# Two packed matmul blocks moved next to each other at the end of four L2 phases

## The chip, the cores and the metric

The kernel runs on one core of one Trainium2 chip. The metric is the device time of one execution in microseconds (us). A run counts as slow when it took over 1.5% longer than the fastest of its kernel, and as fast otherwise. The sets of experiments ran on different chips, so totals are compared only with runs of before in the same rounds.

## The reference

Linear attention with the feature map elu + 1 on 8 batches of 8 heads (576 positions, 64 values per head), then a gated feed-forward block.

```python
q_p, k_p = phi(q), phi(k)                       # phi = elu + 1
kv  = np.einsum('bhsd,bhse->bhde', k_p, v)      # "k.v" below
z   = np.sum(k_p, axis=2)
num = np.einsum('bhsd,bhde->bhse', q_p, kv)     # "q.kv" below
den = np.einsum('bhsd,bhd->bhs', q_p, z)[..., None] + 1e-06
x   = (num / den), heads side by side           # 4608 tokens x 512
out = (silu(x @ w_gate) * (x @ w_val)) @ w_out  # "L1" is the first two products, "L2" the last
```

## The kernel before

The 4608 tokens are handled in 9 groups of 512. For group g, L1 makes 12 blocks of hidden units and L2 multiplies them with w_out. L2 uses the seven-product scheme of fast matrix multiplication. Each product exists twice (`tt` = 0 and 1, two token halves), so L2 is 14 steps of six 128x256 matmuls. Results gather in four half-used PSUM banks. The two "x banks" are `pX[0]`, `pX[1]` and the two "z banks" are `pX[2]`, `pV[2]`. Between the products, VectorE and ScalarE read partial sums out: `k1`, `k2`, `k5` are copies by ScalarE, `c11`, `c22`, `c12` drains by VectorE.

While L2 of group g runs, TensorE also does two small jobs for later groups, as packed 64x64 matmuls (four tiles of the array at once):

- **q.kv** of the next group (`mm2`, 16 matmuls for two batches) fills the four banks `pV[1]`, `pG[1]`, `pV[0]`, `pG[0]`. These are copied to `xT`, which L1 of the next group reads. ScalarE copies two of them and VectorE two.
- **k.v** of the batch after that (`joint`, 72 matmuls) fills parts of two banks, `kvb[b]`. VectorE makes `zd` from them and ScalarE `R`.

```python
    def mm1(b, lp):
        if lp == 0:
            kvb[b] = ((pV[2], pX[0]), (pX[2], pV[2]), (pX[0], pX[1]), (pV[0], pG[0]), (pV[1], pG[1]))[min(b, 4)]
        for j in range(J):
            ...                                   # (cut) for hh in 0, 1
                    for e in range(2):
                        nc.tensor.matmul(
                            out=kvb[b][hh][D * e:D * e + D, 256 * lp:256 * lp + D + 1],
                            lhsT=term_[rows, j, P * lp + D * e:P * lp + D * e + D],
                            rhs=vm[b % 2][rows, j, 2 * lp + e, :], start=(j == 0), stop=(j == J - 1))

    def mm2(g, ps, engs):                         # (cut)
        for b in sorted(set(u[0] for u in us)):
            ...
                corners([x[:, c0:c0 + C * len(js)] for x in ps], kv(b), b, js[0], js[-1] + 1)
        for i in range(4):                        # the xT copies
            ...

    # l2_steps(g), the list of steps for groups 2 to 6: p[n][tt] is product n of half tt
            return [(p[1][0],), (p[1][1], k1[0]), (p[2][0], k1[1]), (p[2][1], c11[0]), (p[6][0], c11[1]),
                    (p[6][1], k2[0]), (p[5][0], k2[1]), (p[5][1], k5[0]), (p[7][0], k5[1]), (p[7][1], c22[0]),
                    (p[3][0], c22[1]), (p[3][1], c12[0], o1[0]), (p[4][0], c12[1], o1[1]), (p[4][1], c21[0], o2[0]),
                    (c21[1], o2[1])]

    # the loop over the steps i
            if i == (7 if g in TS else 8) and b1 < NG:
                mm2(b1, (pV[1], pG[1], pV[0], pG[0]), "AVAV")     # q.kv behind p[7][0]
            ...
            if i == 10 and b2 < B:
                joint(b2)                                         # k.v behind p[3][0]
```

## Time and profile before

| | before |
|---|---|
| median of 3 runs | 310.95 us (310.8 to 311.03) |
| span of the profiled run, granted clock | 308.7 us, 0.996 |
| TensorE busy | 97% |
| L2, first L2 matmul to first L1 matmul of the next group, groups 2 / 3 / 4 / 5 | 10.65 / 10.65 / 10.65 / 10.65 us |

The last row is the finest measure. TensorE has no slack there, and it repeats to 0.01 us. The totals scatter by half a microsecond and more. The start of group 2's L2, ahead of anything that is changed here, lay anywhere from 109.66 to 110.81 us in the fourteen profiled runs of this study.

From the page of the kernel before: the busy time of each engine, then the chain that ended last by engine.

```profile
PE 300.2 (97%) x2551; PEld 182.6 (59%) x2551; DVE 252.7 (82%) x536; ACT 218.5 (71%) x336; POOL 48.5 (16%) x62
...
PE 84%; issue 5%; DMA 3%; POOL 2%; ACT 2%; DVE 2%; POOLq 0%
```

The chain is TensorE's by 84%, so what counts is TensorE's own list of work.

The timeline of TensorE's weight loads at the end of L2 in group 4. Columns: start us, length us, engine, line of the program, operation, what is loaded, shape, count, and in brackets the idle time before it and what ended it. L271 is q.kv, L189 is k.v, L513 the products of L2, L298 L1.

```profile
179.23 0.42 PEld L271 LDWEIGHTS <-R 64*64 64x64 f16 x16 [0.21 <-issue]
179.79 1.21 PEld L513 LDWEIGHTS <-hs 128*128 128x128 f16 x12
181.21 0.67 PEld L189 LDWEIGHTS <-kp 64*64 64x64 f16 x72 [0.21 <-DVE xT L287]
181.92 0.55 PEld L513 LDWEIGHTS <-hs 128*128 128x128 f16 x6
182.48 1.30 PEld L513 LDWEIGHTS <-hT 128*128 128x128 f16 x12
183.79 0.64 PEld L298 LDWEIGHTS <-wg 128*128 128x128 f16 x4
```

The matmuls of the same stretch (the packed ones left out):

```profile
178.49 0.82 PE L513 MATMUL pX<-ws,hs 128*128 128x256 f16 x6
...
179.80 0.83 PE L513 MATMUL pX<-ws,hs 128*128 128x256 f16 x6
180.46 0.82 PE L513 MATMUL pX<-wo,hs 128*128 128x256 f16 x6
...
181.92 0.83 PE L513 MATMUL pV<-wo,hs 128*128 128x256 f16 x6
182.59 1.47 PE L513 MATMUL pX<-ws,hT 128*128 128x256 f16 x12
183.90 1.03 PE L298 MATMUL pG<-xT,wg 128*128 128x512 f16 x4
```

Read it so. One product takes 0.656 us: two in a row are 1.31 us, 182.59 to 183.90. Its matmuls start every 0.109 us. From 178.49 to 179.80 is one product and q.kv, so q.kv costs 0.65 us. From 180.46 to 181.92 is one product and k.v, so k.v costs 0.80 us. Both packed blocks begin after an idle gap of 0.21 us of the weight loader. One gap is filed under "issue" and the other under a VectorE copy.

### The profile page before, as it was taken

To read this page: it belongs to the slowest core of one execution; us is meant where nothing else is said; L and a number is where in the kernel's file an instruction comes from. 1 tells how busy PE (TensorE), PEld (TensorE's weight loads), DVE (VectorE), ACT (ScalarE), POOL (GpSimd) and SP (SyncE) were. 2 spreads that over 40 slices of the span, in tenths; PEclk is the share of its full clock that TensorE was granted. 3 is DMA by queue.
4 is the path that set the end of the run, shared out by engine and by line. 5 is a ranking of instruction groups with operands and counts; after the bars stand their busy time and mean duration, and the time that the engine had idled before them with its cause. 6 is when DMAs were issued, how large, how long until landed. Compare 5 with 4: busy or idle time off the path is not lost.

```text
span 308.7 us, 6601 instructions
## 1 busy us (share of the span) xinstructions
PE 300.2 (97%) x2551; PEld 182.6 (59%) x2551; DVE 252.7 (82%) x536; ACT 218.5 (71%) x336; POOL 48.5 (16%) x62
## 2 busy tenths in 40 slices
PE   8899999999999999999999999999999999999992
PEld 6644453344444476447744674468446888878782
DVE  2757857888967999898989898998899868967981
ACT  3769969859856969696959695969533478548830
POOL 8535286010200002000200000000000004001200
PEclk9999999999999999999999999999999999999998
DMA  7999999997396227921793205120612050032014
GB/s 99 194 200 199 204 207 210 243 229 136 59 244 129 28 51 115 253 54 27 102 233 67 45 21 121 28 51 2 138 25 51 15 124 2 0 79 62 1 38 100
DMA packets 41424, 32.29 MB, mean 105 GB/s; under 512 B 16352, under 2 KB 37280, under 8 KB 41392
## 3 DMA queue, kind: packets, MB, share of 16 engines
q0 software_dynamic: 20672, 18.94, 39.0%
q1 hardware_dynamic: 20560, 12.79, 17.8%
q8 instruction: 20, 0.33, 0.4%
q10 hardware_dynamic: 160, 0.13, 0.2%
q14 instruction: 12, 0.10, 0.1%
HBM read 37.75 MB, written 9.44 MB: 153 GB/s over the span
## 4 chain that ended last, share of the span: by engine, by line
PE 84%; issue 5%; DMA 3%; POOL 2%; ACT 2%; DVE 2%; POOLq 0%
PE pV L298 22%; PE pG L298 22%; PE pX L513 14%; PE pV L513 4%; PE pV L350 4%; PE pG L350 4%; DMA wv<-in_moe_w_val_dram 3%; PE pX L298 3%; PE pG L457 2%; PE pV L457 2%; PE pX L350 1%; PE pV L271 1%; PE pV L418 1%; PE pV L189 1%; DVE osb L467 1%
## 5 line engine op out<-in xcount | busy, mean ns | idle before, releaser
L298 PE MATMUL pV<-xT,wv 128*128 128x512 f16 x324 | 83.5, 379 | 0.2 <-DMA wv<-in_moe_w_val_dram 0.2
L298 PE MATMUL pG<-xT,wg 128*128 128x512 f16 x312 | 80.4, 379 | 0.7 <-DVE osb L467 0.6
L303 ACT ACTIVATE sil<-pG 128x512 f16<-128x512 f32 x78 | 46.4, 598 | 30.1 <-PE pG L298 19.4
L304 DVE SCALAR_TENSOR_TENSOR hT<-pV,sil 128x512 f16<-128x512 f32 x81 | 55.3, 686 | 14.1 <-PE pV L298 7.3
L298 PEld LDWEIGHTS <-wv 128*128 128x128 f16 x336 | 32.7, 98 | 40.3 <-DMA wv<-in_moe_w_val_dram 1.1
L298 PEld LDWEIGHTS <-wg 128*128 128x128 f16 x336 | 32.4, 98 | 39.0 <-issue 1.7
L513 PEld LDWEIGHTS <-hs 128*128 128x128 f16 x336 | 31.8, 98 | 5.3 <-issue 0.9
L390 POOL TENSOR_TENSOR hT<-prod,vm 128x512 f16<-128x512 f16 x6 | 6.9, 1154 | 131.0 <-ACT vm L377 131.0
L513 PEld LDWEIGHTS <-hT 128*128 128x128 f16 x252 | 24.6, 98 | 4.0
L513 PE MATMUL pX<-ws,hs 128*128 128x256 f16 x210 | 26.4, 273 | 0.0
L518 ACT ACTIVATE part<-pX 128x256 f32<-128x256 f32 x35 | 12.8, 381 | 13.2 <-PE pX L513 13.1
L95 POOL DMA_DIRECT2D k<-in_k_dram x7 | 5.4, 778 | 78.9 <-ACT part L518 57.8
L487 DVE TENSOR_TENSOR hs<-hT 128x512 f16<-128x512 f16 (+2 forms) x42 | 17.4, 417 | 0.2
L252 DVE TENSOR_TENSOR qp<-qp,rden 128x768 f16<-128x768 f16 x18 | 17.1, 948 | 0.0
L239 DVE TENSOR_REDUCE den<-prod 128x12 f32<-128x768 f16 x18 | 17.0, 942 | 0.0
L120 ACT ACTIVATE ek<-k 128x1152 f16<-128x1152 f16 x14 | 16.0, 1158 | 0.1
L120 ACT ACTIVATE eq<-q 128x1152 f16<-128x1152 f16 x14 | 15.5, 1158 | 0.0
L513 PE MATMUL pX<-wo,hT 128*128 128x256 f16 x126 | 15.2, 273 | 0.0
L457 PEld LDWEIGHTS <-hT 128*128 128x128 f16 x96 | 8.6, 98 | 10.2 <-issue 0.8
L164 ACT ACTIVATE vm<-v 128x1152 f16<-128x1152 f16 x12 | 14.1, 1178 | 0.0
L523 DVE SCALAR_TENSOR_TENSOR osb<-pX,part 128x256 f32<-128x256 f32 x28 | 11.0, 415 | 2.1 <-PE pX L513 1.9
L457 PE MATMUL pG<-wo,hT 128*128 128x512 f16 x48 | 11.7, 380 | 0.0
(185 smaller groups left out, 536.9 us busy)
## 6 DMA issues: line engine op xcount, KB each, us to landing
out_dram<-osb SPq DMA_DIRECT2D x64, 128.0 KB, 3.8
k<-in_k_dram POOLq DMA_DIRECT2D x7, 576.0 KB, 10.1
q<-in_q_dram POOLq DMA_DIRECT2D x7, 576.0 KB, 11.4
v<-in_v_dram POOLq DMA_DIRECT2D x7, 576.0 KB, 14.0
wg<-in_moe_w_gate_dram POOLq DMA_DIRECT2D x6, 256.0 KB, 11.8
wv<-in_moe_w_val_dram POOLq DMA_DIRECT2D x6, 256.0 KB, 12.0
wo<-in_moe_w_out_dram POOLq DMA_DIRECT2D x3, 512.0 KB, 15.8
out_dram<-osb SPq DMA_DIRECT2D x13, 64.0 KB, 2.0
```

The costliest lines, as they stand in the source:

```text
L120: nc.scalar.activation(out=e[:, s, :], in_=src[b % 2][:, s, :], func=AF.Exp, bias=0.0, scale=1.0)
L164: nc.scalar.activation(out=vm[b % 2][:, :, s, 0:D].rearrange("p j l d -> p l j d"), in_=v16[b % 2][:, s, :].rearrange("p l (j d) -> p l j ...
L239: nc.vector.tensor_reduce(out=den[:, HL * j0:HL * j1], in_=prod[:, 0:j1 - j0, :].rearrange("p j (l d) -> p (j l) d", d=D), axis=AX.X, op=A ...
L252: nc.vector.tensor_tensor(out=qv, in0=qv, in1=rden[:, HL * j0:HL * j1].unsqueeze(2).to_broadcast([P, HL * (j1 - j0), D]), op=ALU.mult)
L298: nc.tensor.matmul(out=ps[:, :], lhsT=src[:, i, P * fb:P * fb + P], rhs=xT[i][g % 2][:, :], start=(i == 0), stop=(i == 3))
L303: nc.scalar.activation(out=s[:, :], in_=pg[:, :], func=AF.Silu, bias=0.0, scale=1.0)
L304: nc.vector.scalar_tensor_tensor(out=hT[g % 2][:, fb, :], in0=pv[:, :], scalar=SC, in1=s[:, :], op0=ALU.mult, op1=ALU.mult)
L350: nc.tensor.matmul(out=dst[:, HN * e:HN * e + HN], lhsT=lhs, rhs=rhs, start=(n in (1, 2, 5) and e == 0 and c == 0), stop=(c == 1), skip_gr ...
L457: nc.tensor.matmul(out=pso[(g, t)][:, :], lhsT=hT[g % 2][:, fb, P * t:P * t + P], rhs=wo[:, fb, :], start=(fb == 0), stop=(fb == FB - 1))
L487: (eng or nc.vector).tensor_tensor(out=o, in0=a, in1=b, op=op)
L513: nc.tensor.matmul(out=(z if n in (2, 3, 5) else x)[:, 0:HD], lhsT=left(f), rhs=right(f), start=(f == 0 and n in (1, 2, 5)), stop=(f == HF ...
L518: nc.scalar.activation(out=part[:, 2 * i + tt, :], in_=(x if from_x else z)[:, 0:HD], func=AF.Copy, bias=0.0, scale=1.0 / SC)
```

## The change

The intent is to spare TensorE one change between full-array and packed matmuls. In groups 2 to 5, q.kv moves from behind `p[7][0]` to behind `p[3][1]`, and k.v follows it straight away. q.kv's banks are then still full, so k.v goes to the two z banks, whose sums the last `c12` drain takes out just then. Both `c12` drains stand ahead of the xT copies in VectorE's list.

```diff
-            kvb[b] = ((pV[2], pX[0]), (pX[2], pV[2]), (pX[0], pX[1]), (pV[0], pG[0]), (pV[1], pG[1]))[min(b, 4)]
+            kvb[b] = ((pV[2], pX[0]), (pX[2], pV[2]), (pX[0], pX[1]), (pV[0], pG[0]), (pX[2], pV[2]))[min(b, 4)]
...
-                    (p[3][0], c22[1]), (p[3][1], c12[0], o1[0]), (p[4][0], c12[1], o1[1]), (p[4][1], c21[0], o2[0]),
-                    (c21[1], o2[1])]
+                    (p[3][0], c22[1]), (p[3][1], c12[0], o1[0], *((c12[1], o1[1]) if g < B - 2 else ())),
+                    (p[4][0], *(() if g < B - 2 else (c12[1], o1[1]))), (p[4][1], c21[0], o2[0]), (c21[1], o2[1])]
...
-            if i == (7 if g in TS else 8) and b1 < NG:
+            if i == (7 if g in TS else 11 if b2 < B else 8) and b1 < NG:
                 mm2(b1, (pV[1], pG[1], pV[0], pG[0]), "AVAV")
...
-            if i == 10 and b2 < B:
+            if i == 11 and b2 < B:
                 joint(b2)
```

## The prediction

> **What bounds the kernel.** TensorE: the page shows it busy 97% of the 308.7 us span; the chain of work that ended last is 84% PE. The four stretches that the change touches (end of L2 in groups 2 to 5) are alike: from the first seventh product of L2 to the first L1 matmul of the next group the timeline shows 5.41 us each time, TensorE busy throughout. Only a shorter TensorE stream, or a shorter wait in it, counts.
>
> **How a stretch runs now** (timeline, group 4). 128x256 matmuls start every 0.109 us, 0.656 us a product. q.kv (16 matmuls, 64x64 tiles) starts 0.20 us after the last full-array start, 0.09 late; the next product starts 0.56 later. k.v (72 matmuls, 64x64) also starts 0.20 after the last full-array start and takes 0.71. The two excursions cost 0.65 + 0.80 = 1.45 us. The Trainium skill, "TensorEngine Tiling (Array Packing)", Key Properties, says that changing the tiling mode drains TensorE; the gaps agree. The gap before k.v is filed under DVE (xT copy, 0.2 us x4), but equals the one before q.kv, filed under issue: I read it as the switch, not the copy.
>
> **What the change does.** Instruction counts stay. q.kv moves behind both third products, k.v straight behind it in the same tiling. One entry (0.09) and one exit are saved. q.kv streams 1,024 columns per quadrant; L1's 512-column matmuls start every 0.216 us, so that is 0.43 of the 0.56, and the exit 0.13. Ideal gain 0.22 us a group, 0.9 in all.
>
> **What takes it back.** k.v now writes the two half banks that the third products just filled, and waits until VectorE drains them. VectorE is in k's phi until 180.50 in group 4 (unchanged, it follows ScalarE's exp). Then come four drains (c22, c22, c12, c12; 0.41 us each, pitch 0.33): starts 180.42, 180.75, 181.08, 181.42, the last ending at 181.83. The last third product would be done at 181.28, so the backlog adds a tenth. With an estimated 0.05 us to be seen, the second bank can be written from 181.88; without a wait k.v could start at 181.64. So 0.24 us of new wait meets 0.22 of saving: the stretch ends at 183.90, where it ends today. Weights loaded during the wait may give back some hundredths.
>
> **The rest stays off the path.** xT copies end later: ScalarE's about 183.0 (behind both q exps), VectorE's about 183.1, against L1's start near 183.9. zd ends about 183.6, R copies 183.4; q's phi starts where it did. The products that now come earlier wait for ScalarE's keeps, which end at 179.49 and 179.76 against 179.80 and 180.46.
>
> **Prediction.** 0.0 to -0.1 us a group: 310.7 us, range 310.0 to 311.3. Faster by over 2%: 0.01; within: 0.98; slower: 0.01.
>
> **What would show it.** Right: stretches within 0.12 us of 5.41 in groups 2 to 5; k.v waiting some 0.2 us for the c12 drain; no full-array matmul between q.kv and k.v; L1 not waiting for xT. Wrong: a stretch near 5.19 (the drain came in time), or over 5.5 (it came later, or L1 waits).
>
> **What would make it wrong.** Drains earlier or at closer pitch; a longer delay from VectorE to TensorE; a TensorE drain between q.kv and k.v although both use 64x64 tiles; q.kv's banks held into L1; a different granted clock (0.996 now).

## The result and the profile after

| | before | after |
|---|---|---|
| median of 6 runs | 310.88 us (310.47 to 311.35) | 311.08 us (310.7 to 311.45) |
| span, granted clock of the profiled run | 308.7 us, 0.996 | 308.9 us, 0.998 |
| TensorE busy | 97% | 97% |
| L2 in groups 2 / 3 / 4 / 5 | 10.65 / 10.65 / 10.65 / 10.65 | 10.65 / 10.64 / 10.65 / 10.65 us |

The ratio is 1.0006, with a 95% interval from 0.9993 to 1.0019: no difference. A ratio is the mean time of one kernel's fast runs over that of the other's of the same rounds, so it is not quite the ratio of the medians quoted.

The busy times and the chain by engine on the page of the changed kernel:

```profile
PE 300.7 (97%) x2551; PEld 183.6 (59%) x2551; DVE 252.5 (82%) x536; ACT 217.5 (70%) x336; POOL 48.4 (16%) x62
...
PE 84%; issue 5%; DMA 4%; POOL 2%; ACT 2%; DVE 2%; POOLq 0%
```

Weight loads in group 4 of the changed kernel (this execution runs 0.28 us later than the one before, already at the start of this L2):

```profile
181.49 0.42 PEld L271 LDWEIGHTS <-R 64*64 64x64 f16 x16 [0.21 <-issue]
181.87 0.11 PEld L189 LDWEIGHTS <-kp 64*64 64x64 f16 x3
182.16 0.64 PEld L189 LDWEIGHTS <-kp 64*64 64x64 f16 x69 [0.18 <-issue]
182.85 1.21 PEld L513 LDWEIGHTS <-hT 128*128 128x128 f16 x12
184.07 0.64 PEld L298 LDWEIGHTS <-wg 128*128 128x128 f16 x4
```

TensorE's matmuls there, with the first of k.v:

```profile
178.77 1.47 PE L513 MATMUL pX<-ws,hs 128*128 128x256 f16 x12
...
181.95 0.20 PE L189 MATMUL pX<-vm,kp 64*64 64x65 f16 x2
182.16 0.22 PE L189 MATMUL pV<-vm,kp 64*64 64x65 f16 x2
...
182.86 1.48 PE L513 MATMUL pX<-ws,hT 128*128 128x256 f16 x12
184.18 1.03 PE L298 MATMUL pG<-xT,wg 128*128 128x512 f16 x4
```

VectorE in the same stretch (L147 is the end of k's phi, L523 the drains, L287 the xT copies):

```profile
180.03 0.76 DVE L147 TENSOR_TENSOR kp<-kp,ek 128x1152 f16<-128x1152 f16 x1
180.70 1.08 DVE L523 SCALAR_TENSOR_TENSOR osb<-pX,part 128x256 f32<-128x256 f32 x3
181.70 0.41 DVE L523 SCALAR_TENSOR_TENSOR osb<-pV,part 128x256 f32<-128x256 f32 x1
182.11 1.29 DVE L287 TENSOR_SCALAR xT<-pG 128x512 f16<-128x512 f32 x2
```

The picture is the predicted one. q.kv and k.v stand together and one 0.21 us gap at a change of shape is gone. But the third k.v matmul, the first into `pV`, starts 0.21 us after the second. The fourth drain ends at 181.70 + 0.41 = 182.11, and that matmul starts at 182.16. From the first seventh product (178.77) to L1 (184.18) it is 5.41 us, as before.

The times fit a wait for the drain, but the profile does not say so: it files the 0.18 us under "issue". So the wait needed a proof.

### The profile page after: what moved, and what is told of

It is laid out like the page before. It is cut to its first block, busy times and chain, and to the rows that moved or that the text cites. A ratio compares the mean times of both kernels' runs of the same rounds, so it can differ in the third digit from the quotient of the medians.

```text
span 308.9 us, 6601 instructions
## 1 busy us (share of the span) xinstructions
PE 300.7 (97%) x2551; PEld 183.6 (59%) x2551; DVE 252.5 (82%) x536; ACT 217.5 (70%) x336; POOL 48.4 (16%) x62
## 4 chain that ended last, share of the span: by engine, by line
PE 84%; issue 5%; DMA 4%; POOL 2%; ACT 2%; DVE 2%; POOLq 0%
PE pV L298 22%; PE pG L298 22%; PE pX L513 14%; PE pV L513 4%; PE pV L350 4%; PE pG L350 4%; DMA wv<-in_moe_w_val_dram 4%; PE pX L298 3%; PE pG L457 2%; PE pV L457 2%; PE pX L350 1%; PE pV L271 1%; PE pV L418 1%; PE pV L189 1%; DVE osb L467 1%
## 5 line engine op out<-in xcount | busy, mean ns | idle before, releaser
L513 PEld LDWEIGHTS <-hs 128*128 128x128 f16 x336 | 32.5, 98 | 4.7 <-DVE hs L487 0.4
L513 PE MATMUL pX<-ws,hs 128*128 128x256 f16 x210 | 25.7, 273 | 0.0
L523 DVE SCALAR_TENSOR_TENSOR osb<-pX,part 128x256 f32<-128x256 f32 x28 | 10.7, 416 | 2.1 <-PE pX L513 1.9
```

The source lines that it names most:

```text
L513: nc.tensor.matmul(out=(z if n in (2, 3, 5) else x)[:, 0:HD], lhsT=left(f), rhs=right(f), start=(f == 0 and n in (1, 2, 5)), stop=(f == HF ...
```

## The experiments

Theory W: k.v waits for the last `c12` drain, and that wait takes back what the spared change of shape gives. The rival, S: the 0.2 us is TensorE finishing q.kv, whatever VectorE does, and there was never anything to win. A third, I (a limit on the supply of instructions), came up on the way.

| experiment | L2 of groups 2 / 3 / 4 / 5, us | median us | ratio to before, 95% |
|---|---|---|---|
| before | 10.65 / 10.65 / 10.65 / 10.65 | 310.7 to 311.2 beside these runs | |
| after | 10.65 / 10.64 / 10.65 / 10.65 | 311.08 | 1.0006 (0.9993 to 1.0019) |
| 1 late drain | 10.98 / 10.99 / 10.98 / 10.98 | 311.97 | 1.0038 (1.0019 to 1.0057) |
| 2 one product later | 10.61 / 10.60 / 10.60 / 10.64 | 310.51 | 0.9991 (0.9973 to 1.0009) |
| 3 the same, table load early | 10.62 / 10.61 / 10.60 / 10.65 | 310.83 | 0.9999 (0.9977 to 1.0021) |
| 4 apart | 11.19 / 11.18 / 11.19 / 11.19 | 313.13 | 1.0070 (1.0052 to 1.0088) |
| 5 drain one place earlier | 10.56 / 10.55 / 10.55 / 10.55 | 310.39 | 0.9978 (0.9956 to 0.9999) |
| 6 old banks | 11.30 / 11.31 / 11.33 / 11.37 | 313.80 | 1.0089 (1.0073 to 1.0105) |
| 7 k.v longer by 16 | 10.78 / 10.78 / 10.78 / 10.78 | one run | |
| 8 k.v longer by 32 | 10.92 / 10.92 / 10.91 / 10.92 | one run | |
| 9 as 5, again | 10.56 / 10.55 / 10.55 / 10.56 | 310.56 | 0.9983 (0.9970 to 0.9997) |
| 10 k.v first | 10.53 / 10.56 / 10.58 / 10.61 | one run | |
| 11 apart, mended | 10.65 / 10.65 / 10.65 / 10.65 | one run | |
| 12 k.v first, q.kv by head pair | 10.44 / 10.45 / 10.44 / 10.44 | 310.01 | 0.9977 (0.9961 to 0.9993) |

All twelve gave correct results. Each L2 is the difference of two starts in the timeline, as in the table of before.

### 1. Hold the drain up on purpose

To the changed kernel:

```diff
+        def slow():
+            nc.vector.tensor_scalar(out=r8[:, :, :], in0=r8[:, :, :], scalar1=1.0, scalar2=None, op0=ALU.min)
...
-                    (p[3][0], c22[1]), (p[3][1], c12[0], o1[0], *((c12[1], o1[1]) if g < B - 2 else ())),
+                    (p[3][0], c22[1]), (p[3][1], c12[0], o1[0], *((slow, c12[1], o1[1]) if g < B - 2 else ())),
```

> The changed kernel with one useless VectorE pass over 512 FP32 columns put ahead of the last drain (c12 of the second half) in groups 2 to 5; I estimate it at 0.35 to 0.6 us of VectorE's time (the 512-column FP16 sums take 0.42). Theory W (k.v waits for that drain): each of the four stretches grows from 5.41 us by about what the pass takes of VectorE's queue, all of it showing as idle between the third and fourth weight load of k.v; total some 1.4 to 2.4 us more than the changed kernel's 311.1, near 312.8. Theory S (the 0.2 us between q.kv and k.v is TensorE finishing q.kv, whatever VectorE does): stretches stay at 5.41 and the total at 311.1.

VectorE in group 4; L553 is the useless pass:

```profile
181.85 0.41 DVE L553 TENSOR_SCALAR r<-r 128x512 f32<-128x512 f32 x1
182.18 0.42 DVE L523 SCALAR_TENSOR_TENSOR osb<-pV,part 128x256 f32<-128x256 f32 x1
```

The weight loads of k.v in the same group:

```profile
182.01 0.11 PEld L189 LDWEIGHTS <-kp 64*64 64x64 f16 x3
182.65 0.64 PEld L189 LDWEIGHTS <-kp 64*64 64x64 f16 x69 [0.52 <-issue]
```

The pass takes 0.33 us of VectorE's queue (181.85 to 182.18), and L2 grows by 0.33 to 0.35 us in all four groups. The growth sits between the third and the fourth weight load. The dose answers one to one, so W is shown and S has fallen. The total, 311.97 us, is below the range given (1.4 to 2.4 us above 311.1). The pass was a little shorter than I had estimated, but four times 0.33 is still 1.3 us and the total shows 0.9. The two totals are not of the same rounds, and scatter by as much as the rest. The profile still files the whole 0.52 us under "issue".

### 2 and 3. One product later, so that the drain is over

```diff
-            if i == (7 if g in TS else 11 if b2 < B else 8) and b1 < NG:
-                mm2(b1, (pV[1], pG[1], pV[0], pG[0]), "AVAV")
+            if i == (7 if g in TS else 12 if b2 < B else 8) and b1 < NG:
+                mm2(b1, (pV[1], pG[0], pV[0], pG[1]) if b2 < B else (pV[1], pG[1], pV[0], pG[0]), "AVAV")
...
-            if i == 11 and b2 < B:
+            if i == 12 and b2 < B:
                 joint(b2)
```

> q.kv and k.v still back to back, but one product later, between the two fourth products, so that the drain is over (about 182.1 in group 4) before k.v comes to it (about 182.6); q.kv's second and fourth bank are exchanged so that L1's first bank comes free first. Theory W: no gap between q.kv and k.v, stretches of 5.19 us instead of 5.41 (0.22 less), L1's first matmuls not waiting; total about 0.9 below before, 310.0. A loss is possible behind the stretch: the R copies and the table load move ScalarE's first silu to about 187.2 in group 4, so that L1's third block may wait 0.2 us a group; then 310.2 to 310.9. Theory S: the gap of 0.2 us stays between q.kv and k.v, stretches 5.41, total 311.

Experiment 3 also loads ScalarE's silu table two steps earlier (`tb` 12 instead of 14).

> As the run before, with the load of the silu table moved to right behind ScalarE's xT copies, where ScalarE would wait for zd anyhow. Theory W: stretches 5.19, first silu of L1 no later than 186.3 in group 4, no wait of L1's third block; total 0.9 below before, about 310.0. Theory S: stretches 5.41, total 311.

The gap between q.kv and k.v is gone in both, as W says. But L2 is 10.60 to 10.65 us where 10.43 was expected (0.22 less than 10.65): only 0.00 to 0.05 us a group is won, least in group 5. TensorE shows a new stop, in all four groups of both kernels: 0.12 to 0.14 us, when 66 or 68 of the 72 k.v matmuls have started. Group 4 of experiment 2:

```profile
183.54 0.20 PE L189 MATMUL pV<-vm,kp 64*64 64x65 f16 x2
183.66 0.22 PE L189 MATMUL pX<-vm,kp 64*64 64x65 f16 x2
183.67 0.22 PE L189 MATMUL pV<-vm,kp 64*64 64x65 f16 x2
183.83 0.28 PE L513 MATMUL pX<-ws,hT 128*128 128x256 f16 x1
```

Pairs of k.v matmuls otherwise start 0.02 us apart. The expectation failed here, and I took a limit on the supply of instructions (theory I) for the reason, to be tested in 7 and 8. The early table load changed nothing that the totals show.

### 4 and 11. The two blocks apart, with the drained banks

q.kv goes back behind `p[7][0]`; k.v stands between the two fourth products, in the z banks.

```diff
-            if i == (7 if g in TS else 11 if b2 < B else 8) and b1 < NG:
+            if i == (7 if g in TS else 8) and b1 < NG:
...
-            if i == 11 and b2 < B:
+            if i == 12 and b2 < B:
                 joint(b2)
```

> q.kv where it was before the change (behind the first seventh product), k.v alone between the two fourth products in the two half banks, which are drained by then. Theory W (saving is the spared change of tiling, about 0.22 us a group, and before's gap of 0.2 ahead of k.v is that change and not the xT copy): two changes of tiling and no drain to wait for, so stretches of 5.41 again, with 0.20 us from the last full-array start to the first k.v load although its banks have been free for half a microsecond; total 310.9. Rival: the gap of before was the wait for the xT copy; then k.v starts about 0.1 us sooner and the stretches are 5.32, total 310.5.

L2 was 11.19 us, 0.54 more than expected. I had overlooked VectorE's order:

```profile
182.03 1.28 DVE L287 TENSOR_SCALAR xT<-pG 128x512 f16<-128x512 f32 x2
183.23 1.07 DVE L523 SCALAR_TENSOR_TENSOR osb<-pX,part 128x256 f32<-128x256 f32 x3
184.22 0.41 DVE L523 SCALAR_TENSOR_TENSOR osb<-pV,part 128x256 f32<-128x256 f32 x1
```

The xT copies stood ahead of the drains. The last drain ended at 184.63, when the third k.v matmul, at 184.69, had been waiting for 0.25 us. The fourth product had already waited 0.32 us, by the times for a `c22` drain (the profile files it under "issue"). The experiment did not take the waits away, so it says nothing of the switch. It only confirms again that k.v follows the drain. Experiment 11 mends it: `mm2` hands its two VectorE copies back, and they are issued behind the four drains.

```diff
+    held = []
...
+                mm2(b1, (pV[1], pG[1], pV[0], pG[0]), "AVAV", hold=b2 < B)
...
+            if i == 11:
+                while held:
+                    held.pop(0)()
```

> The experiment with q.kv and k.v apart, mended: q.kv behind the first seventh product, k.v between the two fourth products in the drained half banks, and VectorE's xT copies put behind the four drains, which they held up before. No wait is left but the two changes of tiling: k.v's first weights 0.20 us behind the last full-array start although its banks have been free for 0.3 us or more, k.v 0.58 from first to last, L2 10.65 us a group as before the change. If before's gap ahead of k.v was the xT copy after all: about 10.55.

The weight loads in group 4, and then VectorE's drains (L528) and copies:

```profile
181.89 0.64 PEld L518 LDWEIGHTS <-hT 128*128 128x128 f16 x6
182.75 0.67 PEld L189 LDWEIGHTS <-kp 64*64 64x64 f16 x72 [0.21 <-issue]
183.46 0.55 PEld L518 LDWEIGHTS <-hT 128*128 128x128 f16 x6
```

```profile
181.55 0.42 DVE L528 SCALAR_TENSOR_TENSOR osb<-pX,part 128x256 f32<-128x256 f32 x1 [0.15 <-PE pX L518]
182.20 0.42 DVE L528 SCALAR_TENSOR_TENSOR osb<-pV,part 128x256 f32<-128x256 f32 x1 [0.23 <-PE pV L518]
```

L2 is 10.65 us, as expected. The banks were free at 181.97 and 182.62, and k.v still began with a gap of 0.21 us, at 182.75 (I had expected both banks to be free 0.3 us ahead; the second was so by 0.13). So the 0.21 us is the change of shape. The page of before had filed the same gap under VectorE's xT copy. The first such copy took 0.68 us from 180.42, so it ended at 181.10, 0.11 us before k.v began; a drain lets k.v go after 0.05 us.

### 5 and 9. The drain one place earlier in VectorE's list

```diff
-                    (p[3][0], c22[1]), (p[3][1], c12[0], o1[0], *((c12[1], o1[1]) if g < B - 2 else ())),
+                    (p[3][0], *(() if g < B - 2 else (c22[1],))),
+                    (p[3][1], c12[0], o1[0], *((c12[1], o1[1], c22[1]) if g < B - 2 else ())),
```

> The changed kernel with VectorE's four drains in the order c22, c12, c12, c22 in groups 2 to 5, so that the one k.v waits for is third instead of fourth. Theory W: that drain then starts when its product is done, about 0.12 us earlier; L2 (first L2 matmul to first L1 matmul) 10.53 us a group instead of 10.65; total 0.5 below the changed kernel, about 310.5, hardly beyond noise. Theory S (the gap is not this wait): 10.65. Theory I (a burst of more than some 165 TensorE instructions runs out of supply, as the 0.12 us stop after the 68th k.v matmul of the run before suggests; a wait ahead of it lets the supply catch up): part of the 0.12 comes back as a stop near the end of k.v, L2 between 10.53 and 10.65.

> The kernel of the run with the drain order c22, c12, c12, c22 once more, with more rounds, because its gain (0.10 us a group in the trace, 0.40 in all, 0.13%) is near the noise of the totals. Expected: L2 10.55 again in groups 2 to 5; total 0.2 to 0.7 below before in the same rounds.

L2 is 10.55 or 10.56 us in every group of both profiles, 0.10 less, and the gap inside k.v is 0.12 to 0.13 instead of 0.21 us. The backlog of VectorE was worth the "tenth" of the prediction. The last `c12` drain and the first k.v matmuls in group 4 of experiment 5:

```profile
181.26 0.42 DVE L523 SCALAR_TENSOR_TENSOR osb<-pV,part 128x256 f32<-128x256 f32 x1
181.61 0.20 PE L189 MATMUL pX<-vm,kp 64*64 64x65 f16 x2
181.74 0.22 PE L189 MATMUL pV<-vm,kp 64*64 64x65 f16 x2
```

The drain now ends at 181.68, and the first matmul into `pV` still follows it by 0.06 us: what is left of the gap is the same wait. Both totals lie below before, by 0.2%, with intervals that end just below 1.

### 6. The old banks, with the new order

```diff
-            kvb[b] = (..., (pX[2], pV[2]))[min(b, 4)]
+            kvb[b] = (..., (pV[1], pG[1]))[min(b, 4)]
```

> The changed kernel with k.v in the two banks it had before the change (the ones that q.kv has just filled), the order kept. Theory W (k.v waits for whatever drains its banks): it waits for the xT copies, which end about 0.68 us after the drain that the changed kernel waits for; L2 11.3 us a group instead of 10.65, total near 313.8. Theory S: 10.65, total 311.

L2 is 11.30 to 11.37 us, as W says. Without the half banks the new order would have lost 0.65 to 0.72 us a group.

### 7 and 8. Is it the supply of instructions?

To the kernel before, 16 or 32 of the k.v matmuls are done twice (n = 4 or 8); each repeated group is closed and restarted.

```diff
-        for j in range(J):
+        for (j, end) in ([(j, n - 1) for j in range(n)] if b > 3 and lp == 0 else []) + [(j, J - 1) for j in range(J)]:
...
-                            rhs=vm[b % 2][rows, j, 2 * lp + e, :], start=(j == 0), stop=(j == J - 1))
+                            rhs=vm[b % 2][rows, j, 2 * lp + e, :], start=(j == 0), stop=(j == end))
```

> The kernel before the change (k.v alone, full-array products ahead of it) with 16 k.v matmuls of groups 2 to 5 done twice (restarted, so the result stays): 88 matmuls, 176 instructions with their weight loads, as long a burst as q.kv and k.v together (also 88). At the rate of before, 72 in 0.58 us, they take 0.71 from first to last. Theory I (supply of instructions): a stop of about 0.12 us after some 82 to 84 matmuls, 0.83 in all. Rival N (the stop belongs to the neighbourhood of q.kv, or to that place in the list): no stop, 0.71.

> As the run before with 32 k.v matmuls done twice: 104 matmuls, 208 instructions. Without a stop 0.84 us from first to last. Theory I: the same stop after some 82 to 84 matmuls and 0.96 or more in all. Rival N: 0.84.

From the first to the last k.v matmul it was 0.71 us with 88 of them and 0.84 to 0.85 with 104, with no stop. Theory I, as it was stated, has fallen: a burst longer than q.kv and k.v together runs at full rate. (The total of run 7, 310.0 us, is below before although its L2 is longer. Its group 2 began early, at 109.66 us: a warning about single totals.)

### 10. k.v ahead of q.kv

From experiment 3, with the k.v matmuls issued ahead of `mm2`, and `zd` and `R` behind it:

```diff
+            if i == 12 and b2 < B:
+                for lp in range(2):
+                    mm1(b2, lp)
             if i == (7 if g in TS else 12 if b2 < B else 8) and b1 < NG:
...
             if i == 12 and b2 < B:
-                joint(b2)
+                for lp in range(2):
+                    zdiag(b2, lp)
+                r_copies(b2)
```

> k.v ahead of q.kv, both between the two fourth products, the silu table loaded early as in the run of that name. The supply of instructions is refuted, so what stops TensorE for 0.12 us before the last four k.v matmuls when q.kv goes ahead is open. If it comes with k.v running straight behind q.kv, it is absent here: k.v 0.58 us from first to last, and from the first k.v to the last fourth product 1.14 to 1.17 us instead of 1.33. If it comes with any burst of 88 of these small matmuls or with this place in the list, it stays: some 1.3. The xT copies then end about 0.6 us later, so L1 should wait 0.1 to 0.2 us for them; the total is no better than before's 310.9.

From the first packed matmul to the last fourth product it is 1.16 or 1.17 us, against 1.32 to 1.36 in experiment 2 and 1.32 to 1.37 in experiment 3. The stop is gone, and the place in the list is the same, so it goes with the order of the two blocks. What makes it when q.kv goes first stays open. As expected, L1 then waits for an xT copy, and the profile names it this time (list of waits of the weight loader: who waited for whom, us in total, times, the longest):

```profile
PEld L298 <- DVE xT L287: 1.0, 4, 0.3
```

### 12. The same, with q.kv finished bank by bank

q.kv now does the first head pair of both batches, then the second, so that two of its banks are ready half-way. The banks are given out in the order in which L1 takes them.

```diff
-        for b in sorted(set(u[0] for u in us)):
+        bs = sorted(set(u[0] for u in us))
+        for (lps, b) in [(x, b) for x in ((0,), (1,)) for b in bs] if by_lp else [((0, 1), b) for b in bs]:
...
-                mm2(b1, (pV[1], pG[0], pV[0], pG[1]) if b2 < B else (pV[1], pG[1], pV[0], pG[0]), "AVAV")
+                mm2(b1, (pG[0], pV[0], pG[1], pV[1]) if b2 < B else (pV[1], pG[1], pV[0], pG[0]), "AVAV", b2 < B)
```

> As the run with k.v ahead of q.kv (its L2 was 10.53 to 10.61 us, because L1 then waited 0.09 to 0.17 us for the xT copies), with q.kv ordered so that its first two banks are complete half-way (both batches of the first head pair, then both of the second) and the banks given out in the order in which L1 takes them. The first two copies can then start some 0.2 us sooner and L1 should not wait: L2 10.42 to 10.45 us a group, 0.2 below both kernels, that is the whole of the spared change of tiling; total 0.8 to 0.9 below before in the same rounds, near 310.2, if nothing in L1 waits for the later zd and R copies. If L1 still waits, 10.5 and more.

The weight loads in group 4 (L514 is the products of L2, L299 is L1):

```profile
180.57 0.64 PEld L514 LDWEIGHTS <-hT 128*128 128x128 f16 x6
181.42 0.68 PEld L189 LDWEIGHTS <-kp 64*64 64x64 f16 x72 [0.21 <-issue]
182.01 0.38 PEld L271 LDWEIGHTS <-R 64*64 64x64 f16 x16
182.58 0.55 PEld L514 LDWEIGHTS <-hT 128*128 128x128 f16 x6 [0.20 <-issue]
183.15 0.64 PEld L299 LDWEIGHTS <-wg 128*128 128x128 f16 x4
```

One change of shape in, one out, and no wait between. (The last drain ended at 181.39 here, only 0.03 us before k.v began, so this place is only just late enough.) L2 is 10.44 or 10.45 us: 0.20 to 0.21 less than before (and than after, within 0.01), the whole of the spared change. The median is 310.01 us against 310.71 of the ten fast runs of before in the same rounds, 0.70 us less. By the ratio it is 0.7 us, with an interval from 0.2 to 1.2; four times 0.21 is 0.84 and lies inside. (The eleventh run of before in that set took 800.38 us. It is not a fast run and is left out.) This version beats the kernel before by 0.2%. It was not timed in the same rounds as the changed kernel; against that one only the L2 times speak.

## Why the prediction was right

The prediction was 310.7 us (310.0 to 311.3), "within 2%". Measured: 311.08. The total alone proves little. The full saving without any wait, four times 0.22 us, would have given about 310.0, which also lies in the range. What tells the two apart is L2, which kept its 10.65 us. Point by point:

- **TensorE bounds these stretches.** Right: every change of L2 in the traces came from TensorE's list or from a wait or stop in it.
- **The gap ahead of k.v in the kernel before is the change of shape, not the xT copy.** Right: experiment 11 (one run) keeps the 0.21 us with both banks free. The Trainium skill, "TensorEngine Tiling (Array Packing)", Key Properties, says that a change of tiling mode drains TensorE. This agrees: 0.20 us instead of 0.109 on the way in, and on the way out 0.13 to 0.14 from the start of the last k.v matmul to that of the next full-array one.
- **One spared change is worth 0.22 us a group.** Right as the bound that it was: experiment 12 gets 0.20 to 0.21. But the prediction priced it for q.kv ahead of k.v. With that order, one product later and without the wait (experiments 2 and 3), a stop inside k.v leaves 0.00 to 0.05. So I was right that the wait takes the saving back. I did not foresee that, at a place without it, this order would keep at most a quarter of the saving. Whether the stop would also come at the predicted place is not shown, as k.v waits there in every run.
- **A new wait of about 0.24 us for the c12 drain takes it back.** Right: 0.21 us in the trace, proved by experiments 1, 5 and 6. The four drains came at the pitch and place that were predicted, and the estimate of 0.05 us from drain to matmul fits (182.11 to 182.16).
- **Stretches stay at 5.41 us.** Right, 5.41 in group 4.
- **The rest stays off the path.** Right in effect: L1 does not wait. One term was off. The R copies were to end at 183.4 in group 4; they end at 184.44, or 184.16 without the 0.28 us of shift. ScalarE waited 0.83 us for VectorE's `zd`, which reads the same banks. The Trainium skill, "PSUM — Partial Sum Buffer", Terms, says that ScalarE and VectorE may not read one bank and quadrant at once. The order seen here agrees; no run tried to break it.

The small gain in the point (0.2 us below before) is not there: the medians differ by 0.2 us the other way, inside the noise of the totals.

## What to carry to other kernels

When a move makes one engine's list shorter, ask which buffer the moved work now needs and who frees it: here VectorE's queue gave a new wait as long as the saving, and neither a busy share nor the list of waits showed it. The name beside a gap is a guess, so test it with a dose: add a known delay to the suspected engine and see whether the gap grows by just that. Where two blocks are to be joined, try both orders, and price the order by what each one's consumers and buffers need next.

## What the Trainium skill lacked or had wrong

- "TensorEngine Tiling (Array Packing)", Key Properties, says that a change of tiling mode drains TensorE but gives no cost. Here a 64x64 block among 128x128 matmuls costs about 0.09 us on the way in (0.20 against a pitch of 0.109). On the way out, 0.13 to 0.14 us pass from the start of the last k.v matmul to that of the next full-array one. Sparing one such pair saves 0.20 to 0.21 us.
- No page that I read tells of the stop of 0.12 to 0.14 us near the end of 72 packed matmuls that follow 16 longer packed ones in the same mode (experiments 2 and 3), which is absent when the order is turned (experiment 10) and with 104 of them alone (experiment 8). Its cause is open.
- "Perfetto Trace Analysis", Per-instruction lifecycle, says that waits fall outside the profiled window. A reader should be told besides that the cause filed beside a gap, which the reading tool infers, can fail in both directions: 0.2 us filed under a VectorE copy that was a change of mode (before, experiment 11), and 0.52 us filed under "issue" that was a wait for VectorE (experiment 1).
